# Attention of a linear-attention and feed-forward kernel rebuilt: one projection stretch a unit, four changes of array form a period

## The chip, the cores and the metric

The kernel runs on one core of one Trainium2 chip. The metric is device time in microseconds, taken as the median of three runs. The engines are TensorE (in the profile PE for matmuls and PEld for weight loads), VectorE (DVE), ScalarE (ACT), GpSimd (POOL) and SyncE (SP, which here only issues DMAs). Each engine works through its own instructions in program order and waits on semaphores for the others.

## The reference

There are 64 pairs of batch and head, with 576 positions of width 64. Keys and queries go through the same feature map, and the attention is linear: its cost grows with the sequence, not with its square. The result is rearranged to 4608 tokens of width 512 and goes through a feed-forward part whose gate is h - tanh(h).

```python
def phi(x):
    proj = np.einsum('bhsd,df->bhsf', x, w_phi)                   # d = 64, f = 128
    proj = proj - np.max(np.abs(proj), axis=-1, keepdims=True)
    return np.concatenate([np.exp(proj), np.exp(-proj)], axis=-1) # 256 features
q_p, k_p = phi(q), phi(k)
kv  = np.einsum('bhsf,bhsd->bhfd', k_p, v)
z   = np.sum(k_p, axis=2)
num = np.einsum('bhsf,bhfd->bhsd', q_p, kv)
den = np.einsum('bhsf,bhf->bhs', q_p, z)[..., None] + 1e-06
x   = (num / den), rearranged to (4608, 512)
h   = x @ w_in                                                    # (512, 2048)
out = (h - np.tanh(h)) @ w_out                                    # (2048, 512)
```

The feed-forward weights arrive as 64-bit floats and are turned to 32-bit floats on the chip ("decode").

## The kernel before, in words

**Units.** Two heads of one batch entry form a unit, so there are 32 units. For each, queries and keys stand transposed and side by side in one tile `qk` (64 rows for each head, 1152 columns: nine tiles of 128 positions). Tiles 0 to 3 and half of tile 4 are queries; the other half of tile 4 and tiles 5 to 8 are keys.

**Steps of a unit.** `project` multiplies the nine tiles by `w_phi`; the two heads sit in the upper and lower 64 rows of the array and run side by side, into the two halves (banks) of a PSUM tile. `centre` takes, on VectorE, the maximum of the absolute values over the features (`m`) and subtracts it (`t`). Keys then go through the two exponentials on ScalarE (`k_exp`, tile `kp`). Queries are first transposed on TensorE (`q_turn` and, for the half tile, `q_turn_rest`) and then go through the exponentials (`q_exp`, `q_exp_rest`, tile `qe`). `kv` multiplies keys and values (tile `pc`); its result is copied (`kv_copy`), transposed (`kv_turn`) and copied again (`kv_turn_copy`, on VectorE). `kadd` adds the key features over the five position tiles on GpSimd (tile `ss`); `ksum` adds over the 128 rows with a matmul by ones (tile `pu`), and the sum is copied, transposed and copied (`ksum_copy`, `ksum_turn`, `ksum_turn_copy`). `num` and `denom` are the products with the query features. `denom`'s result goes to memory and back in another layout (`den_recip_load`), is inverted on VectorE (`den_recip`), stored, spread over 64 rows by DMA (`den_spread`), multiplied into the numerator on GpSimd (`den_mul`) and stored (`x_store`).

**Array forms.** `project` uses the array as two tiles of 64 rows; `kv` and `num` as two of 64 columns; `denom` and `ksum` as four of 32 columns; transposes use it whole. In the profile's rows the form stands as `64*128`, `128*64`, `128*32` or `128*128`.

**Order.** `period(i)` writes the order out by hand: inside it every engine executes in the order in which the code calls. A period works on several units: unit i is projected, unit i-1 (`c`) gets its key exponentials, `kv` and query transposes, unit i-2 (`p`) its `num` and `denom`, units i-3 and i-4 the division. One weight tile is decoded in each period (`dec_0` on ScalarE, `dec_1` to `dec_3` on VectorE, in the second bank of the tile `pt`), and for 14 of them the split into a high and a low part is made too (`split_w`). The projection is in two stretches: tiles 0 to 4 at the period's start (0 to 3 into `pj`'s two banks, 4 into `pt`), tiles 5 to 8 after `kv` (into the same `pj`). The half-tile query transposes are written into `pt` as well. A first run of 16 warm-up matmuls stands ahead of unit 0's projection, a second of 16 in period 1. After 33 periods, `last` finishes the last unit, and the feed-forward part follows.

**PSUM.** Eight banks: `pj` two, `po` two single ones (used by the query transposes and by `num` in turn), `pt` two, `pc` and `pu` one each.

Of the kernel before, what the change touches and what calls it, by code (L numbers as in the profile page):

```python
# [32 lines left out]
def tile_linear_attention_moe(  # L33
# [90 lines left out]
    with ExitStack() as c1:  # L124
# [5 lines left out]
        ps_d = c1.enter_context(tc.tile_pool(name="ps_d", bufs=2, space=PSUM))  # L130
# [72 lines left out]
        def project(u, r):  # L203
            if r == 0:
                u.pt = ps_t.tile([P, 2, 512], F32, tag="pt", name=f"pt{u.i}")
                n, j0 = 5, 0
            else:
                n, j0 = 4, 5
            if (u.i, r) == (0, 1):
                pp = [ps_c.tile([P, 512], F32, tag=g, name=f"pp{u.i}_{r}_{g}") for g in ("pc", "pu")]  # L210
                u.x = [(slice(e, e + 1), slice(0, n), pp[e].rearrange("p (e a f) -> p e a f", e=1, f=F)) for e in range(2)]
            else:
                t = ps_pj.tile([P, 2, 512], F32, tag="pj", name=f"pp{u.i}_{r}")
                pp = [t[:, e, :] for e in range(2)]
                x = t.rearrange("p e (a f) -> p e a f", f=F)
                cut = (0, 4) if u.i else (0, 2, 4)
                u.x = [(slice(0, 2), slice(a0, a1), x[:, :, a0:a1]) for a0, a1 in zip(cut, cut[1:])]
                if r == 0:
                    last = (slice(0, 2), slice(4, 5), u.pt[:, :, 0:F].rearrange("p e (a f) -> p e a f", a=1))
                    u.x.insert(0 if u.i else 2, last)  # L220
            for a in range(n):
                for e in range(2):
                    hs = slice(e * D, (e + 1) * D)
                    o = u.pt[:, e, 0:F] if a == 4 else pp[e][:, a * F : (a + 1) * F]
                    nc.tensor.matmul(o, u.qk[hs, (j0 + a) * P : (j0 + a + 1) * P], wph[hs, :], start=True, stop=True)  # L225
            u.m = p2.tile([P, 2, n], F32, tag=f"m{r}", name=f"m{u.i}_{r}")
            u.t[r] = p2.tile([P, 2, n, F], F32, tag=f"t{r}", name=f"t{u.i}_{r}", bufs=1 if r else 2)

        def absmax(u, k):
            e, a, x = u.x[k]  # L230
            nc.vector.tensor_reduce(u.m[:, e, a], x, AX.X, ALU.max, apply_absolute_value=True)

        def less_max(u, r, k):
            e, a, x = u.x[k]
            m = u.m[:, e, a].unsqueeze(3).broadcast_to([P, e.stop - e.start, a.stop - a.start, F])
            nc.vector.tensor_tensor(u.t[r][:, e, a], x, m, ALU.subtract)  # L236

        def centre(u, r):
            for k in range(len(u.x)):
                absmax(u, k)  # L240
                less_max(u, r, k)

        def q_turn_rest(u, pt):
            for e in range(2):
                nc.tensor.transpose(pt[:, 0, (2 + e) * P : (3 + e) * P], u.t[0][:, e, 4, :], ident)

        def q_turn(u, e):
            pt = ps_d.tile([P, 512], F32, tag="po", name=f"ptt{u.i}_{e}")
            for j in range(4):
                nc.tensor.transpose(pt[:, j * P : (j + 1) * P], u.t[0][:, e, j, :], ident)  # L250
            return pt

        def q_exp_rest(u, pt):
            x = pt[:, 0, 2 * P : 4 * P].rearrange("p (e t) -> p e t", e=2)[:, :, 0:SR]
            for s in range(2):
                nc.scalar.activation(u.qe[:, :, s, SM:S], x, AF.Exp, scale=1.0 - 2.0 * s)

        def q_exp(u, e, pt):
            for s in range(2):
                nc.scalar.activation(u.qe[:, e, s, 0:SM], pt, AF.Exp, scale=1.0 - 2.0 * s)  # L260

        def k_exp(u, r):
            h, x, j = ((slice(SR, P), 4, 0), (slice(0, P), slice(0, 4), slice(1, 5)))[r]
            for s in range(2):
                nc.scalar.activation(u.kp[h, :, j, s, :], u.t[r][h, :, x, :], AF.Exp, scale=1.0 - 2.0 * s)  # L265
# [13 lines left out]
        def kadd(u):  # L279
            x = p1.tile([P, 2, 2, F], F32, tag="ss", name=f"ss{u.i}")  # L280
# [6 lines left out]
        def ksum(u):  # L287
            parts = [u.ss] if u.ss is not None else [u.kp[:, :, j] for j in range(5)]
            for a, x in enumerate(parts):
                for n in range(4):  # L290
                    nc.tensor.matmul(
                        u.pu[n * 32 : (n + 1) * 32, 0:F], ones, x[:, n // 2, n % 2, :], start=(a == 0), stop=(a == len(parts) - 1)
# [6 lines left out]
        def ksum_turn(u, bank, n=0):  # L299
            u.pz = bank[:, n * F : (n + 1) * F]  # L300
            nc.tensor.transpose(u.pz, u.kst, ident)

        def ksum_turn_copy(u):
            u.ks = p2.tile([P, P], F32, tag="ks", name=f"ks{u.i}")
            nc.scalar.copy(u.ks, u.pz)
# [9 lines left out]
        def num(u):  # L315
            u.po = [ps_d.tile([P, 512], F32, tag="po", name=f"po{u.i}_{c}") for c in range(2)]
            for s in range(2):
                for c in range(2):
                    for e in range(2):
                        nc.tensor.matmul(  # L320
                            u.po[c][e * D : (e + 1) * D, 0:CH],
# [20 lines left out]
        def num_copy(u):  # L342
            u.d = tail.tile([P, S], F32, tag="d", name=f"d{u.i}", bufs=2)
            for c in range(2):
                nc.scalar.copy(u.d[:, c * CH : (c + 1) * CH], u.po[c][:, 0:CH])
# [10 lines left out]
        def den_recip(u, pin=lambda ins: ins):  # L356
            w = 2 * S // P
            u.rr = dr.tile([2, S], F32, tag="rr", name=f"rr{u.i}")
            rn = tail.tile([P, w], F32, tag="rn", name=f"rn{u.i}")
            pin(nc.vector.reciprocal(rn, u.dn))  # L360
            nc.sync.dma_start(u.rr.rearrange("a s -> (a s)").rearrange("(p c) -> p c", c=w), rn)
# [14 lines left out]
        for i in range(B * NHP):  # L376
            u = Unit()
            u.i, u.b, u.hp = i, i // NHP, i % NHP
            u.t, u.ss, u.kp = {}, None, kps[i % 2]
# [6 lines left out]
        nc.scalar.dma_start(wph[D:P, :], w_phi)  # L386
        load_v(units[0])
        load(units[1])
        dec = [dec_load(0), dec_load(1)]

# [3 lines left out]
        def q_all(c, pt):  # L394
            c.qe = p2.tile([P, 2, 2, S], F32, tag="qe", name=f"qe{c.i}")
            pts = [q_turn(c, e) for e in range(2)]
            q_turn_rest(c, pt)
            if c.i:
                kv_turn(c)
            for e in range(2):  # L400
                q_exp(c, e, pts[e])
            q_exp_rest(c, pt)

        def period(i):
            a, c, p, r, q = (unit(i - n) for n in range(5))
            w = dec[i - 2] if 2 <= i < NU + 2 else None
            if q:
                den_mul(q)
                x_store(q)
            if i == NU - 2:  # L410
# [3 lines left out]
            if a:  # L414
                if i == 0:
                    warm(16, "pc")
                project(a, 0)
                pt = a.pt
                centre(a, 0)
            else:  # L420
                pt = ps_t.tile([P, 2, 512], F32, tag="pt", name=f"pt{i}")
            if i == 1:
                q_all(c, a.pt)
                warm(16, "pu")
            if p:
                num(p)
            if c:
                k_exp(c, 1)
                if i < NU:
# [267 lines left out]
```

## Time and profile before

| | us |
|---|---|
| median of three runs | 1133.14 (1131.47 to 1135.79) |
| the profiled execution | 1134.21, its span 1132.1 |
| start to the second `num` (unit 1) | 34.30 |
| from there to the `num` of unit 29, 28 periods | 277.84 |
| from there to the first feed-forward matmul | 28.49 |
| feed-forward part to the end of the span | 791.47 |

The profile is of one execution, and its times count from the start of the span. A row of the timeline is: start, length from the first to the last of a merged run, engine, line, operation, names of output and inputs, shapes, how often. A matmul of 32-bit floats leaves two records. The length of a merged run of matmuls holds the run-out of its last one, so the distance from one row's start to the next row's start says how long the array was taken. In brackets stands the idle time of the engine ahead of the run and what ended it.

### The profile page before, as it was taken

To read this page: it belongs to the slowest core of one execution; us is meant where nothing else is said; L and a number is where in the kernel's file an instruction comes from. 1 tells how busy PE (TensorE), PEld (TensorE's weight loads), DVE (VectorE), ACT (ScalarE), POOL (GpSimd) and SP (SyncE) were. 2 spreads that over 40 slices of the span, in tenths; PEclk is the share of its full clock that TensorE was granted. 3 is DMA by queue.
4 is the path that set the end of the run, shared out by engine and by line. 5 is a ranking of instruction groups with operands and counts; after the bars stand their busy time and mean duration, and the time that the engine had idled before them with its cause. 6 is when DMAs were issued, how large, how long until landed. Compare 5 with 4: busy or idle time off the path is not lost.

```text
span 1132.1 us, 18798 instructions
## 1 busy us (share of the span) xinstructions
PE 1109.2 (98%) x7008; PEld 872.2 (77%) x7008; DVE 835.6 (74%) x1170; ACT 778.9 (69%) x1488; POOL 432.3 (38%) x345
## 2 busy tenths in 40 slices
PE   7999999999979999999999999999999999999997
PEld 5666676666647888888888888888888888888885
DVE  5888888888858877767767767667676776776664
ACT  4887887777757766666666666666666666666664
POOL 4678876666634552322222222222222222222222
PEclk9999999999999999999999999999999999999999
DMA  4666767767731001101002002002002002000001
GB/s 158 179 191 212 217 207 210 208 200 216 224 103 38 1 27 48 33 21 65 1 1 75 1 1 75 1 1 75 1 1 75 1 1 75 1 1 29 10 0 38
DMA packets 51163, 85.46 MB, mean 75 GB/s; under 512 B 13312, under 2 KB 24960, under 8 KB 51072
## 3 DMA queue, kind: packets, MB, share of 16 engines
q1 hardware_dynamic: 50912, 84.20, 24.0%
q8 instruction: 55, 0.90, 0.3%
q14 instruction: 36, 0.29, 0.1%
q10 hardware_dynamic: 160, 0.07, 0.0%
HBM read 65.08 MB, written 19.02 MB: 74 GB/s over the span
## 4 chain that ended last, share of the span: by engine, by line
PE 87%; DMA 4%; POOL 3%; DVE 2%; ACT 2%; issue 1%; SPq 1%; POOLq 0%; DVEq 0%; ACTq 0%
PE ph L538 34%; PE po L581 11%; PE po L584 11%; PE po L582 11%; PE pp L225 4%; PE po L320 4%; PE pc L271 4%; PE pu L334 2%; DMA rb<-rr 2%; PE ptt L250 2%; DMA rr<-rn 2%; PE pt L225 1%; DMA dn<-dd 1%; POOL ss L282 1%; POOL ss L281 1%
## 5 line engine op out<-in xcount | busy, mean ns | idle before, releaser
L567 POOL TENSOR_TENSOR gl<-s,gh 128x512 fp32r<-128x512 f32 x144 | 186.1, 1293 | 556.2 <-ACT gh L566 547.7
L545 ACT ACTIVATE y<-ph 128x512 f32<-128x512 f32 x144 | 86.1, 598 | 254.9 <-PE ph L538 254.9
L554 DVE SCALAR_TENSOR_TENSOR s<-s,y 128x512 f32<-128x512 f32 x144 | 102.3, 711 | 187.4 <-ACT s L547 186.4
L581 PE MATMUL po<-who,gh 128*128 128x512 f32 x572 | 222.8, 389 | 1.8 <-ACT gh L566 1.8
L538 PE MATMUL ph<-xh,whi 128*128 128x512 f32 x576 | 224.3, 389 | 0.0
L538 PE MATMUL ph<-xh,wli 128*128 128x512 f32 x576 | 224.1, 389 | 0.0
L538 PE MATMUL ph<-xl,whi 128*128 128x512 f32 x576 | 224.1, 389 | 0.0
L582 PE MATMUL po<-wlo,gh 128*128 128x512 f32 x572 | 222.5, 389 | 0.0
L584 PE MATMUL po<-who,gl 128*128 128x512 f32 x572 | 152.9, 389 | 0.0
L560 DVE COPY_PREDICATED s<-mk,th 128x512 f32<-128x512 uint32 x128 | 122.9, 960 | 13.8 <-DVE th L559 0.9
L581 PEld LDWEIGHTS po<-who,gh 128*128 128x128 f32 x572 | 107.4, 188 | 24.9 <-ACT gh L566 2.6
L538 PEld LDWEIGHTS ph<-xh,whi 128*128 128x128 f32 x576 | 108.3, 188 | 23.3 <-DVE s L560 0.5
L538 PEld LDWEIGHTS ph<-xh,wli 128*128 128x128 f32 x576 | 108.1, 188 | 22.5
L538 PEld LDWEIGHTS ph<-xl,whi 128*128 128x128 f32 x576 | 108.1, 188 | 22.3
L582 PEld LDWEIGHTS po<-wlo,gh 128*128 128x128 f32 x572 | 107.4, 188 | 22.2
L584 PEld LDWEIGHTS po<-who,gl 128*128 128x128 f32 x572 | 107.3, 188 | 22.3
L547 ACT ACTIVATE s<-y,bias_t 128x512 f32<-128x512 f32 x144 | 104.4, 725 | 0.4 <-POOL gl L567 0.4
L553 ACT ACTIVATE mk<-y,bias_t 128x512 f32<-128x512 f32 x144 | 103.5, 719 | 1.4 <-DVE s L560 1.4
L557 DVE SCALAR_TENSOR_TENSOR s<-s,ph 128x512 f32<-128x512 f32 x144 | 98.9, 687 | 5.2
L556 DVE SCALAR_TENSOR_TENSOR s<-s,s 128x512 f32<-128x512 f32 x128 | 88.8, 694 | 16.2 <-ACT s L549 3.5
L265 ACT ACTIVATE kp<-t 128x1024 f32<-128x1024 f32 (+1 forms) x128 | 86.8, 727 | 14.5 <-DVE t L236 12.7
L549 ACT ACTIVATE s<-y,bias_t 128x512 f32<-128x512 f32 x128 | 92.4, 722 | 0.9 <-POOL gl L567 0.9
(101 smaller groups left out, 1708.6 us busy)
## 6 DMA issues: line engine op xcount, KB each, us to landing
qk<-in_qkT SPq DMA_DIRECT2D x31, 576.0 KB, 4.8
v<-in_v SPq DMA_DIRECT2D x32, 320.0 KB, 3.2
rb<-rr SPq DMA_DIRECT2D x64, 144.0 KB, 3.2
xs<-rb SPq DMA_DIRECT2D x32, 288.0 KB, 3.5
out<-o SPq DMA_DIRECT2D x36, 256.0 KB, 2.0
rawi<-in_moe_w_in SPq DMA_DIRECT2D x16, 512.0 KB, 3.9
rawo<-in_moe_w_out SPq DMA_DIRECT2D x16, 512.0 KB, 6.2
xl<-xs SPq DMA_DIRECT2D x24, 256.0 KB, 4.0
```

The lines of the kernel that those rows point to most:

```text
L538: nc.tensor.matmul(h, wt[:, c * P : (c + 1) * P], x[:, c, 0:N], start=(i == 0), stop=(i == 3 * NCT - 1))
L547: nc.scalar.activation(s1, y, AF.Square, bias=bias_t[:, 0:1])
L549: nc.scalar.activation(s2, y, AF.Square, bias=bias_t[:, 1:2])
L553: nc.scalar.activation(mk, y, AF.Relu, bias=bias_t[:, 2:3])
L554: nc.vector.scalar_tensor_tensor(s1, s1, PC1, y, ALU.add, ALU.mult)
L556: nc.vector.scalar_tensor_tensor(gs, s2, PC2, s1, ALU.add, ALU.mult)
L557: nc.vector.scalar_tensor_tensor(gs, gs, PA, h, ALU.mult, ALU.mult)
L560: nc.vector.copy_predicated(gs, mk.bitcast(U32), hh)
L567: pin(nc.gpsimd.tensor_tensor(gl, gs, f32(gh), ALU.subtract))
L581: nc.tensor.matmul(po[t], a, wo[f][0], start=(f == 0), stop=False)
L582: nc.tensor.matmul(po[t], a, wo[f][1], start=False, stop=False)
L584: nc.tensor.matmul(po[t], gl[:, t * P : (t + 1) * P], wo[f][0], start=False, stop=(f == NF - 1))
```

## The change

The code of the 32 units is written anew; the feed-forward part, and the order of its instructions on each engine, stay as they are.

- `project` takes a list of parts, "j" (tiles 0 to 3, into `pj`), "a" (tiles 5 to 8, into the two-bank tile `po`) and "t" (tile 4, into `pt`). A period from 4 on projects j, a and t without another step between them; period 3 in the order a, j, t.
- `num` writes one two-bank tile `po` and stands at the period's end, right behind `kv`. Its copy (`num_copy`) is one instruction. The query transposes go to `pj`, the half-tile ones to `pu`.
- `ksum_turn`, `denom`, `ksum` and the half-tile transposes of one period share a tile `pu`. `denom` is now for unit i-3 and `ksum` for unit i-2; `kadd`'s tile has two buffers.
- `q_exp` is two instructions over both heads instead of four.
- The decode's three VectorE steps stand at the period's end, behind the reciprocal; each weight tile is decoded one period later than before.
- On SP a period issues: spread of the reciprocals, v, q and k, load of the denominators, store of the reciprocals, store of x, raw weights.
- `ramp` holds the order of the first three units, `drain` that of the end. The first warm-up has 12 matmuls, the second is gone. The first unit's q and k come in two pieces instead of three. In `drain` the last unit's key sum goes through `kadd` like the others.

On TensorE, one period before (`pp` and `pt` are projection, `ptt`, `pt<-ident` and `pc<-ident` transposes, `pu<-qe` is `denom`, `pu<-ss` `ksum`):

```order
L225 MATMUL pp_0_1235<-wph,qk_1034 128x128 x8
L225 MATMUL pt_1234<-wph,qk_1034 128x128 x2
L320 MATMUL po_0_1252<-qe_1187,kv_1210 64x288 x2
...
L271 MATMUL pc_1281<-kp_113,v_1020 64x256 x10
L225 MATMUL pp_1_1308<-wph,qk_1034 128x128 x8
L301 MATMUL pu_1319<-ident,kst_1271 128x128
L250 MATMUL ptt_0_1324<-ident,t_0_1111 128x128 x4
...
L245 MATMUL pt_1234<-ident,t_0_1111 128x128 x2
L309 MATMUL pc_1281<-ident,kvt_1300 128x128 x2
L334 MATMUL pu_1319<-qe_1187,ks_1321 32x288 x8
```

and one period of the change:

```order
L219 MATMUL pj_1276<-wph,qk_1035 128x128 x8
L219 MATMUL pa_1285<-wph,qk_1035 128x128 x8
L219 MATMUL pt_1294<-wph,qk_1035 128x128 x2
L341 MATMUL pu<-qe_1084,ks_1220 32x288 x8
L299 MATMUL pu<-ss_1172,ones 32x128 x4
L316 MATMUL pc_1227<-ident,kvt_1238 128x128 x2
L247 MATMUL ptt_1334<-ident,t_0_1142 128x128 x8
L308 MATMUL pu<-ident,kst_1327 128x128
L252 MATMUL pu<-ident,t_0_1142 128x128 x2
L278 MATMUL pc_1358<-kp_114,v_1140 64x256 x10
L327 MATMUL po_1384<-qe_1215,kv_1331 64x288 x8
```

The second projection stretch has moved up to the first, `num` behind `kv`, and the transpose of `kv`'s result to the next period.

On ScalarE, in the same period of the change, from the copy of `denom` to the key exponentials that follow `num`'s copy (`kp<-t_0` and `kp<-t_1` are key exponentials, `pt<-rawi` is the decode's first step):

```order
L355 ACTIVATE dd_1192<-pu,bias_t 128x288
L305 COPY kst_1196<-pu 128x128
L171 ACTIVATE pt_1163<-rawi_989 128x512
L258 ACTIVATE qe_1215<-ptt_1203 128x2x512 x2
L267 ACTIVATE qe_1215<-pu 128x2x64 x2
L312 COPY ks_1220<-pu 128x128
L272 ACTIVATE kp_114<-t_0_1142 64x2x128 x2
L284 COPY kvt_1238<-pc_1227 128x256
L272 ACTIVATE kp_114<-t_1_1222 128x2x4x128
L351 COPY d_1262<-po_1253 128x576
L272 ACTIVATE kp_114<-t_1_1222 128x2x4x128
```

and in a period before, where the key exponentials stand ahead of the copy and in one piece:

```order
L265 ACTIVATE kp_114<-t_1_2134 128x2x4x128 x2
L265 ACTIVATE kp_113<-t_0_2199 64x2x128 x2
L297 COPY kst_2223<-pu_2135 128x128
L171 ACTIVATE pt_2186<-rawi_2046 128x512
L345 COPY d_2226<-po_0_2204 128x288
L345 COPY d_2226<-po_1_2205 128x288
L277 COPY kvt_2252<-pc_2233 128x256
```

The copy of `num` has moved between the two long key exponentials of the unit that was just projected.

The diff, without the new `ramp` and `drain` past their heads:

```diff
-        ps_d = c1.enter_context(tc.tile_pool(name="ps_d", bufs=2, space=PSUM))
+        ps_d = c1.enter_context(tc.tile_pool(name="ps_d", bufs=1, space=PSUM))
...
-            cut = (0, PC) if u.i else (0, 2 * P, 5 * P, PC)
+            cut = (0, PC) if u.i else (0, 4 * P, PC)
...
+        def project(u, parts):
+            for part in parts:
+                if part == "j":
...
+                    u.pj = ps_pj.tile([P, 2, 512], F32, tag="pj", name=f"pj{u.i}")
+                    bank, tiles = u.pj, range(4)
+                elif part == "t":
+                    u.pt = ps_t.tile([P, 2, 512], F32, tag="pt", name=f"pt{u.i}")
+                    bank, tiles = u.pt, range(4, 5)
+                else:
+                    u.pa = ps_d.tile([P, 2, 512], F32, tag="po", name=f"pa{u.i}")
+                    bank, tiles = u.pa, range(5, 9)
+                for k, a in enumerate(tiles):
+                    for e in range(2):
+                        hs = slice(e * D, (e + 1) * D)
+                        nc.tensor.matmul(
+                            bank[:, e, k * F : (k + 1) * F], u.qk[hs, a * P : (a + 1) * P], wph[hs, :], start=True, stop=True
+                        )
...
+        def centre(u, parts):
+            for part in parts:
+                x, m, t = part_of(u, part)
+                nc.vector.tensor_reduce(m, x, AX.X, ALU.max, apply_absolute_value=True)
+                nc.vector.tensor_tensor(t, x, m.unsqueeze(3).broadcast_to(list(t.shape)), ALU.subtract)
...
+        def num(u, pool=ps_d, tag="po"):
+            u.po = pool.tile([P, 2, 512], F32, tag=tag, name=f"po{u.i}")
...
         def num_copy(u):
             u.d = tail.tile([P, S], F32, tag="d", name=f"d{u.i}", bufs=2)
-            for c in range(2):
-                nc.scalar.copy(u.d[:, c * CH : (c + 1) * CH], u.po[c][:, 0:CH])
+            nc.scalar.copy(u.d.rearrange("p (c n) -> p c n", c=2), u.po[:, :, 0:CH])
...
+        def ramp():
+            a, b, c = units[0:3]
+            warm(12, "pc")
+            project(a, "jat")
...
         def period(i):
             a, c, p, r, q = (unit(i - n) for n in range(5))
-            w = dec[i - 2] if 2 <= i < NU + 2 else None
+            w = dec[i - 3]
+            low = split_w(i - 4) if 4 <= i < 2 * AHEAD + 4 else None
+            if q:
+                den_spread(q)
+            if i > 3:
+                load_v(a)
+            project(a, "jat" if i > 3 else "ajt")
+            if i + 2 < NU:
+                load(units[i + 2])
+            centre(a, "jt")
+            kadd(c)
             if q:
                 den_mul(q)
+            if low:
+                low()
+            pu = bank()
+            if r:
+                denom(r, pu)
+            ksum(p, pu)
+            if r:
+                denom_copy(r)
+                den_recip_load(r)
+            ksum_copy(p)
+            kv_turn(p)
+            kv_turn_copy(p)
+            dec_0(w, a.pt)
+            q_turn(c)
+            ksum_turn(p)
+            q_turn_rest(c, pu)
+            q_exp(c)
+            q_exp_rest(c)
+            ksum_turn_copy(p)
+            centre(a, "a")
+            k_exp(a, 0)
+            kv(c)
+            kv_copy(c)
+            k_exp(a, 1, (0,))
+            if r:
+                den_recip(r)
+                den_store(r)
+            if q:
                 x_store(q)
+            dec_1(w)
+            dec_2(w)
+            dec_3(w)
+            dec.append(dec_load(i - 1))
...
+            num(p)
+            num_copy(p)
+            k_exp(a, 1, (1,))
...
+        def drain():
+            q, r, p, c = units[-4:]
+            kadd(c)
...
+            kv(c)
+            num(p)
...
+            kv_turn(c)
...
+            ksum(c, pu)
+            denom(p, pu)
...
+            ksum_turn(c)
...
+            num(c)
...
+            denom(c, bank())
+            denom_copy(c)
```

More of the change, by code (lines that the diff above doesn't have):

```diff
@@ L243, in q_turn_rest @@
[L243 to L254, printed above, removed]
+        def project(u, parts):
+            for part in parts:
+                if part == "j":
+                    u.t = [p2.tile([P, 2, 5, F], F32, tag="t0", name=f"t{u.i}_0"), None]
+                    u.m = [p2.tile([P, 2, 5], F32, tag="m0", name=f"m{u.i}_0"), p2.tile([P, 2, 4], F32, tag="m1", name=f"m{u.i}_1")]
+                    u.pj = ps_pj.tile([P, 2, 512], F32, tag="pj", name=f"pj{u.i}")
[12 more added lines that the diff above has]
+                        )
@@ L386, in tile_linear_attention_moe, with bank @@
         nc.scalar.dma_start(wph[D:P, :], w_phi)
+        load(units[1])
         load_v(units[0])
-        load(units[1])
-        dec = [dec_load(0), dec_load(1)]
+        load_v(units[1])
+        dec = []
         def unit(i):
             return units[i] if 0 <= i < NU else None
[L394 to L402, printed above, removed]
+        def bank():
+            return ps_c.tile([P, 512], F32, tag="pu", name="pu")
@@ new lines, in ramp @@
+        def ramp():
+            a, b, c = units[0:3]
+            warm(12, "pc")
+            project(a, "jat")
+            load(c)
+            dec.extend(dec_load(n) for n in range(2))
+            centre(a, "jta")
+            k_exp(a, 0)
+            q_turn(a, ("pc", "pu"))
+            q_turn_rest(a, a.pt[:, 0])
+            project(b, "j")
+            q_exp(a)
+            q_exp_rest(a)
+            k_exp(a, 1)
+            project(b, "at")
+            load(units[3])
+            centre(b, "jta")
+            kadd(a)
+            q_turn(b)
+            k_exp(b, 0)
+            kv(a)
+            load_v(c)
+            q_turn_rest(b, b.pt[:, 0])
+            q_exp(b)
+            kv_copy(a)
+            q_exp_rest(b)
+            kv_turn(a)
+            kv_turn_copy(a)
+            project(c, "jat")
+            load(units[4])
+            k_exp(b, 1)
+            centre(c, "jta")
+            kadd(b)
+            pu = bank()
+            ksum(a, pu)
+            ksum_copy(a)
+            kv(b)
+            load_v(units[3])
+            kv_copy(b)
+            ksum_turn(a)
+            ksum_turn_copy(a)
+            k_exp(c, 0)
+            k_exp(c, 1, (0,))
+            num(a, ps_pj, "pj")
+            num_copy(a)
+            k_exp(c, 1, (1,))
@@ L413, in period @@
                     x_load(0, xt[0], j)
[L414 to L429, printed above, removed]
-                    kadd(c)
@@ L500, in last, with decode @@
+        def decode(w):
+            pt = ps_t.tile([P, 2, 512], F32, tag="pt", name="pt")
+            dec_0(w, pt)
             dec_1(w)
@@ L507, in tile_linear_attention_moe @@
         with tc.manual_schedule():
-            for i in range(NU + 1):
+            ramp()
+            for i in range(3, NU):
                 period(i)
-            last()
-        den_recip_load(units[-2])
-        den_mul(units[-3])
-        x_store(units[-3])
+            drain()
         den_recip_load(units[-1])
```

209 lines of the change are left out of this document (88 added, 121 removed).

## The prediction

> **What bounds the kernel now.** I read the page first, then the windows by stage, then one period of the attention engine by engine. On the page, the busy times and the chain that ended last:
>
> ```profile
> PE 1109.2 (98%) x7008; PEld 872.2 (77%) x7008; DVE 835.6 (74%) x1170; ACT 778.9 (69%) x1488; POOL 432.3 (38%) x345
> ...
> PE 87%; DMA 4%; POOL 3%; DVE 2%; ACT 2%; issue 1%; SPq 1%; POOLq 0%; DVEq 0%; ACTq 0%
> ```
>
> TensorE is the bound nearly everywhere. By stages (length, then busy time of PE, PEld, DVE, ACT, POOL, then granted clock), cut at the second `num`, at that of unit 29 and at the first matmul of the feed-forward part:
>
> ```profile
> 34.30:312.14 277.84, 274.84 (x3055) 190.41 (x3053) 243.21 (x336) 220.44 (x492) 197.25 (x153) 1.00 0.69 207
> 312.14:340.63 28.49, 22.03 (x229) 13.58 (x228) 14.50 (x22) 17.11 (x40) 9.27 (x7) 0.94 0.35 102
> 340.63:1132.10 791.47, 785.15 (x3460) 648.39 (x3456) 557.20 (x783) 525.19 (x926) 213.61 (x164) 1.00 0.07 25
> ```
>
> The last row is 70% of the span; its instructions and their order stay, so I leave it at 791.5. The first row is 28 periods of 277.84/28 = 9.92 us each. The second is the drain, with 6.5 us of idle TensorE. Now one period on TensorE (start, length, work):
>
> ```profile
> 200.35 1.18 PE L334 MATMUL pu<-qe,ks 128*32 128x288 f32 x16
> 201.34 0.40 PE L291 MATMUL pu<-ss,ones 128*32 128x128 f32 x8
> 201.67 1.16 PE L225 MATMUL pp<-wph,qk 64*128 64x128 f32 x16
> 202.85 0.49 PE L225 MATMUL pt<-wph,qk 64*128 64x128 f32 x4
> 203.27 2.16 PE L320 MATMUL po<-qe,kv 128*64 128x288 f32 x16
> 205.26 2.33 PE L271 MATMUL pc<-kp,v 128*64 128x256 f32 x20
> 207.52 1.16 PE L225 MATMUL pp<-wph,qk 64*128 64x128 f32 x16
> 208.62 0.33 PE L301 MATMUL pu<-ident,kst 128*128 128x128 f32 x1
> 208.78 1.04 PE L250 MATMUL ptt<-ident,t 128*128 128x128 f32 x8
> ...
> 209.88 0.38 PE L309 MATMUL pc<-ident,kvt 128*128 128x128 f32 x2
> 210.19 1.18 PE L334 MATMUL pu<-qe,ks 128*32 128x288 f32 x16
> ```
>
> The array forms are in the column with the star: 32-column, 64-row, 64-column, 64-row, full, 32-column: five changes in 9.84 us.
>
> **Price of a change of form.** The pace inside one form shows in unit 0's second projection, first and last of eight pairs, and above them the first projection of all:
>
> ```profile
> 4.62 1.16 PE L225 MATMUL pp<-wph,qk 64*128 64x128 f32 x16
> ...
> 5.83 0.27 PE L225 MATMUL pp_pc<-wph,qk 64*128 64x128 f32 x1
> ...
> 6.62 0.27 PE L225 MATMUL pp_pc<-wph,qk 64*128 64x128 f32 x1
> ```
>
> Seven steps in 0.79 us are 0.112 a pair, so eight pairs need 0.89; the stretch at 207.52 takes 1.10 to the next start. Entering and leaving the form cost 0.21. Likewise two transposes at 209.88 take 0.31 to the next start where the ten before them run at 0.11 each: 0.09 for that change.
>
> **The period after.** Projection is one stretch (18 pairs, 2.02), then `denom` and `ksum`, 13 transposes, `kv` and `num`; four changes. Against 9.84: the second stretch's 0.21 goes. In the first stretch ten pairs, 1.12, should with entry and exit take 1.31; they take 1.60 (201.67 to 203.27). The 0.29 between is a wait, and DVE shows for what:
>
> ```profile
> 201.31 0.41 DVE L313 COPY kv<-pc 128x256 f32<-128x256 f32 x1
> 202.02 0.69 DVE L183 SCALAR_TENSOR_TENSOR wo<-rawo,pt 128x512 uint32<-128x512 uint32 x1 [0.29 <-ACT qe L256]
> 203.38 0.42 DVE L231 TENSOR_REDUCE m<-pt 128x2 f32<-128x256 f32 x1 [0.68 <-PE pt L225]
> ...
> 204.18 1.22 DVE L231 TENSOR_REDUCE m<-pp 128x8 f32<-128x1024 f32 x1
> 205.43 1.23 DVE L236 TENSOR_TENSOR t<-pp,m 128x1024 f32<-128x1024 f32 x1
> 206.57 0.20 DVE L360 RECIPROCAL rn<-dn 128x9 f32<-128x9 f32 x1
> ```
>
> The decode's last step (L183) ends at 202.71, held by the exponentials that read the same tile; the projection into `pt` starts at 202.85. In the change those exponentials read `pu`, and tile t comes last in the stretch, so this wait should go. TensorE's own work is then 9.84 - 0.21 - 0.29 = 9.34.
>
> But three hand-overs now lie inside the round. I count from T, the first projection matmul. TensorE: part a at T+1.0, t at 1.9, `denom` 2.2, `kv_turn` 3.6, `q_turn` 3.8, `kv` 5.1, `num` 7.3, next T at 9.3. DVE starts when part j is complete, T+1.2, and steps as above: maximum 1.25, subtraction 1.14, the pair for t 0.80, `kv` copy 0.33 and again 1.25 + 1.2. Part j's bank is empty at T+3.7, with 0.1 to TensorE at 3.8, exactly when `q_turn` wants it; part a's at T+7.2, when `num` wants it. Reciprocal and decode end at T+10.0, 1.2 ahead of the next t. ScalarE:
>
> ```profile
> 202.26 2.82 ACT L265 ACTIVATE kp<-t 128x1024 f32<-128x1024 f32 x4
> ...
> 205.39 0.67 ACT L171 ACTIVATE pt<-rawi 128x512 f32<-128x512 f32 x1
> 205.98 0.70 ACT L345 COPY d<-po 128x288 f32<-128x288 f32 x2
> 207.64 0.37 ACT L277 COPY kvt<-pc 128x256 f32<-128x256 f32 x1 [0.96 <-PE pc L271]
> 208.98 0.27 ACT L305 COPY ks<-pu 128x128 f32<-128x128 f32 x1 [0.97 <-PE pu L301]
> 209.42 2.06 ACT L260 ACTIVATE qe<-ptt 128x512 f32<-128x512 f32 x4 [0.17 <-PE ptt L250]
> 211.34 0.48 ACT L256 ACTIVATE qe<-pt 128x128 f32<-128x128 f32 x2
> ```
>
> From t's subtraction (done T+4.5) it runs decode 0.67, `q_exp` 2.06, the rest 0.48, 0.27, the first three key exponentials (some 1.8 of the 2.82), 0.37, less about 0.6 of overlap (2.06 from 209.42 ends 0.14 past 211.34): T+9.5. `num` is done at 9.4. The copy out of `po`, about 0.65 as one instruction, ends at T+10.15, 0.85 into the next round, where part a wants that bank at 1.0. So all three meet within 0.1. A bank's hand-over costs 0.14 (202.71 to 202.85). None missed: 9.34; each missed by 0.14: 9.76. I take 9.45, a third of the way, because the rows I count with already hold their latencies. 28 x (9.92 - 9.45) = **13.2 us**, bounds 4.5 and 16.2. Every 0.1 us in this figure is 2.8 us in the end. POOL carries what it carries now, 197.25/28 = 7.0 us a period, and its key sum has until the next period's `ksum` instead of the same one's. Of the moved transfers, the spread of the reciprocals is issued on SP behind the raw weights, whose load waits for the decode's end at T+10.0, so at T+1.3 of the next round; POOL wants it after its sums, at about T+6.8, and ScalarE the buffer that POOL then frees at T+9.4. The loads of q, k and v behind it are for units one and two rounds away. I cost these at nothing, since 5 us of POOL's sums cover the spread; without that cover POOL's product, then the copy out of `po`, would come late.
>
> **The ramp.** It is a chain through DVE. Unit 0's part j is complete at 4.62 + 1.16 = 5.8, as now; its centring takes 2.39 + 0.80 + 2.39, to 11.4; unit 1's j to 13.8; `q_turn` 1.0, ScalarE's 2.0 beside `kv` 2.3, copy and turn 0.8, so unit 2 is projected from 17.9 and complete at 19.0, centred at 24.6. Key exponential 1.0 and copy 0.7: 26.4, where unit 3's j finds its bank free. It is complete at 27.6 and centred at 33.5, where the second `num` starts; it is 34.30 now. With hand-overs I call it equal: **0**, bounds 2 gained and 3 lost.
>
> **The drain.** From unit 29's `num`: its 2.0, `denom` and `ksum` 1.3, transposes 1.6, `kv` 2.2, `num` 2.0, `kv_turn` 0.35, `ksum` and `denom` 1.3, turning the last sum 0.9, `num` 2.0, `denom` 1.1: 14.75, with 1 us for waits 15.7 against 28.49. What goes is in these rows:
>
> ```profile
> 322.70 0.42 PE L291 MATMUL pu<-ss,ones 128*32 128x128 f32 x8 [2.20 <-POOL ss L284]
> ...
> 332.24 0.47 PE L301 MATMUL pt<-ident,kst 128*128 128x128 f32 x1 [3.38 <-DVE pt L179]
> 332.51 1.91 PE L250 MATMUL ptt<-ident,t 128*128 128x128 f32 x8
> ```
>
> These three rows hold 5.6 us of waiting, and the last one a halved clock (1.91 for what took 1.04), good for 1.7. Of the busy time, unit 30's `kv` 2.26, its transposes 1.57 and one projection stretch 1.10 now stand ahead of the cut, and the last unit's key sum is made by POOL, which leaves 4 matmuls instead of 20 (some 1.0 at 0.05 each). Together 13.2, near the 12.8 of the two sums. Gain **12.8**, bounds 13.7 (no waits at all) and 8 (the old waits of 5.6 stay, less what is covered). POOL's last sum can start when ScalarE has unit 31's keys, 3.7 after the cut, takes 5.1 and is wanted at 9.4; without these 0.6 us of cover TensorE waits.
>
> **Sum.** -13.2 + 0 - 12.8 = -26.0. The profiled execution took 1134.21 us (span 1132.1), the median run 1133.14, 1.1 less: 1107 to 1108.
>
> **Rivals.**
>
> 1. The hand-overs bind: DVE's ring and TensorE wait for each other and the period is 9.75. For it: no slack in three places; against it: the sums are worked from rows with latency. 28 x 0.17 = 4.8, drain 10: about 1118.
>
> 2. The ramp runs at half clock. It drops the second warm-up and 4 of the first 16.
>
> ```profile
> 21.24 0.63 PE L291 MATMUL pu<-ss,ones 128*32 128x128 f32 x8 [1.98 <-POOL ss L284]
> 21.80 2.08 PE L225 MATMUL pp<-wph,qk 64*128 64x128 f32 x16
> ...
> 21.80:24.23 2.43, 2.43 (x24) 2.21 (x20) 0.03 (x1) 1.74 (x2) 0.56 (x1) 0.50 0.18 72
> ```
>
> After 1.98 us of idleness the clock is 0.50 and sixteen projections take 2.08 instead of 1.16. By the chain above TensorE waits in the new ramp from 6.8 to 8.3, from 10.5 to 11.5 and from 12.6 to 13.9, each shorter than this one. If two of them bring a halved stretch as long as here, about 3 us, some 1.5 is lost in each: 1111. The Trainium skill, "TensorE: Matmul & The Clock Gate", section "Why this matters for your kernels", asks for no idle gap over about 3 us; by that rule no wait of this ramp would slow the clock and the ramp stays at my number, but the row at 21.24 speaks against it.
>
> 3. Slower: the reciprocal waits for its DMA. It stands ahead of the decode on DVE, and now its load is issued behind the spread, v and the next q and k:
>
> ```profile
> 202.40 0.59 SPq L354 DMA_DIRECT2D dn<-dd  x1
> ...
> DVE rn L360 <- DMA dn<-dd: 1.2, 2, 0.8
> ```
>
> Now 4.2 us from issue to use (202.40 to 206.57) cover it, with two waits in 28 periods. Then it is issued at T+4.1 and wanted at T+7.1: 3.0, plus DVE's 0.5 of idle time. Landing after 5 us would stretch every period by 1.5, to 10.95: 28 x 1.03 = 29 lost, 13 gained in the drain: 1150. It turns the whole slower from about 4.4 us on. Against it: q and k's load was in flight in these rows too.
>
> **Chances.** Forecast 0.58 (own range 1101 to 1114), hand-overs 0.23, clock 0.10, reciprocal 0.06, others 0.03. Range 1099 (period 9.34, ramp 2 better, drain at its bound) to 1122 (period 9.76, drain 8). A measurement here tells 0.5% from no change; faster by more 0.91, within 0.03, slower 0.06.
>
> **What would show it.** Projection rows of 16, 16 and 4 back to back, without a gap ahead of `pt`; four forms a period; starts of `num` 9.4 to 9.5 us apart. Waits of TensorE on DVE ahead of `q_turn` or `num` mean rival 1; a clock of 0.50 between 8 and 26 us rival 2; DVE idle ahead of the reciprocal rival 3. First `num` of unit 1 near 34, first feed-forward matmul near 315. It is wrong if the period stays above 9.7 or the drain above 20.

## Result: slower by 2.7%, where 2.2% faster was forecast

The changed kernel takes 1164.65 us (median of four runs, 1163.37 to 1165.66), the kernel before 1133.28 beside it: a ratio of 1.0275, interval 1.0252 to 1.0297. The prediction was 1108, range 1099 to 1122. Of its three rivals the third, to which it gave 0.06, is what happened.

Windows of the changed kernel, cut at the same places as before (length, then busy time of PE, PEld, DVE, ACT, POOL with instruction counts, granted clock, DMA share, GB/s):

```profile
37.80:351.58 313.78, 277.77 (x3055) 187.51 (x3054) 243.59 (x336) 213.19 (x407) 199.04 (x153) 0.99 0.60 181
351.58:370.31 18.73, 16.32 (x150) 8.81 (x149) 11.60 (x19) 11.88 (x25) 8.74 (x7) 0.91 0.54 149
370.31:1162.30 791.99, 785.22 (x3460) 648.18 (x3456) 558.80 (x786) 526.59 (x928) 214.04 (x165) 1.00 0.07 25
```

| us | before | predicted | changed | best repair (below) |
|---|---|---|---|---|
| start to the second `num` | 34.30 | 34.3 | 37.80 | 34.81 |
| 28 periods | 277.84 | 264.6 | 313.78 | 264.21 |
| one period | 9.92 | 9.45 | 11.21 | 9.44 |
| drain | 28.49 | 15.7 | 18.73 | 17.90 |
| feed-forward | 791.47 | 791.5 | 791.99 | 791.88 |
| span | 1132.1 | 1106 | 1162.3 | 1108.8 |

Most of the loss is in the second row: 35.9 us more in 28 periods; 3.5 more go in the ramp, and 9.8 are gained in the drain. In the 28 periods TensorE was busy for 274.84 of 277.84 us before; now it idles for 36. The chain that ended last, on the page of the changed kernel:

```profile
PE 72%; DMA 14%; DVE 10%; ACT 2%; issue 1%; SPq 1%; POOL 0%; POOLq 0%; ACTq 0%; DVEq 0%
```

DMA went from 4% to 14% of it, and 12% is `dn`, the load of the denominators, 4.5 KB a period. The waits in the 28 periods (total, how often, longest):

```profile
DVE rn L365 <- DMA dn<-dd: 59.4, 27, 3.3
...
PE pt L219 <- DVE wi L183: 20.7, 13, 2.2
```

Before there were two such waits of the reciprocal, of 1.2 us together; now it waits in 27 of 28 periods, 2.2 us each. One turn, on VectorE, then SP, then TensorE:

```profile
218.11 0.21 DVE L365 RECIPROCAL rn<-dn 128x9 f32<-128x9 f32 x1 [2.68 <-DMA dn<-dd]
...
220.42 0.69 DVE L183 SCALAR_TENSOR_TENSOR wi<-rawi,pt 128x512 uint32<-128x512 uint32 x1
...
225.86 1.23 DVE L236 TENSOR_TENSOR t<-pa,m 128x1024 f32<-128x1024 f32 x1
229.18 0.21 DVE L365 RECIPROCAL rn<-dn 128x9 f32<-128x9 f32 x1 [2.10 <-DMA dn<-dd]
```

```profile
221.17 0.38 SPq L159 DMA_DIRECT2D rawi<-in_moe_w_in  x1
221.60 2.12 SPq L375 DMA_DIRECT2D rb<-rr  x2
223.82 0.53 SPq L200 DMA_DIRECT2D v<-in_v  x1
224.45 0.38 SPq L196 DMA_DIRECT2D qk<-in_qkT  x1
224.92 0.59 SPq L360 DMA_DIRECT2D dn<-dd  x1
```

```profile
230.22 1.06 PE L219 MATMUL pa<-wph,qk 64*128 64x128 f32 x16
232.23 0.49 PE L219 MATMUL pt<-wph,qk 64*128 64x128 f32 x4 [0.94 <-DVE wo L183]
```

The turn closes on itself. The reciprocal at 218.11 lets the decode run to its end at 221.1. That frees the raw weights' buffer, so SP issues their load at 221.17 (3.06 later), then spread, v, q and k without a pause, and `dn` at 224.92 (3.75 later). The next reciprocal starts at 229.18 (4.26 later). 3.06 + 3.75 + 4.26 = 11.07, where TensorE needs 9.4. TensorE pays at the projection into `pt`: it shares the tile with the decode, and the decode stands behind the late reciprocal.

### The profile page after: what moved, and what is told of

The parts are those of the page before. It is cut to its first block, busy times and chain, and to the rows that moved or that the text cites. A ratio compares the mean times of both kernels' runs of the same rounds, so it can differ in the third digit from the quotient of the medians.

```text
span 1162.3 us, 18558 instructions
## 1 busy us (share of the span) xinstructions
PE 1109.3 (95%) x6956; PEld 866.5 (75%) x6956; DVE 837.1 (72%) x1166; ACT 771.1 (66%) x1394; POOL 439.2 (38%) x349
## 4 chain that ended last, share of the span: by engine, by line
PE 72%; DMA 14%; DVE 10%; ACT 2%; issue 1%; SPq 1%; POOL 0%; POOLq 0%; ACTq 0%; DVEq 0%
PE ph L599 33%; DMA dn<-dd 12%; PE po L642 11%; PE po L645 11%; PE po L643 11%; PE pu L341 2%; DVE pt L179 2%; DVE pt L176 2%; DVE t L236 1%; DVE m L235 1%; DVE pt L175 1%; PE pt L219 1%; DVE wi L183 1%; DVE wo L183 1%; PE pc L316 1%
## 5 line engine op out<-in xcount | busy, mean ns | idle before, releaser
L272 ACT ACTIVATE kp<-t 128x1024 f32<-128x1024 f32 (+1 forms) x128 | 90.5, 731 | 11.7 <-DVE t L236 10.5
```

## The experiments

Two theories. A: the period is long because the reciprocal, ahead of the decode on VectorE, waits for `dn`. B: the hand-overs of banks between TensorE, VectorE and ScalarE bind (the prediction's first rival), and the wait for `dn` only fills slack. Ratios are to the kernel before on the same chip; a period is the time from unit 1's `num` to unit 29's, divided by 28.

### The wait taken away

```diff
-            pin(nc.vector.reciprocal(u.rn, u.dn))
+            pin(nc.vector.reciprocal(u.rn, cd if u.i < NU - 4 else u.dn))
```

`cd` is a tile that is filled once with a constant, so this kernel leaves out the division by the true denominators.

> The reciprocal of all but the last four units reads a tile filled once with a constant instead of the loaded denominators; the load is still issued, and everything else stands as in the change. It leaves out the division by the true denominators, so that only VectorE's wait for that load is gone. Theory A (the changed kernel is slow because the reciprocal, which stands ahead of the decode on VectorE, waits for its load): the period falls from 11.21 to 9.4-9.6 us, the time from 1164.6 to 1114-1121. Theory B (the hand-overs of banks between TensorE, VectorE and ScalarE bind, and the wait for the load is only where the slack is spent): the period stays above 10.5 and the time above 1143.

Measured: 1114.41 us, ratio 0.9812 (0.9783 to 0.9840). The 28 periods, and one of them on TensorE:

```profile
38.36:302.69 264.33, 264.19 (x3055) 183.55 (x3054) 243.32 (x336) 211.40 (x407) 198.80 (x153) 1.00 0.72 215
```

```profile
200.73 1.16 PE L221 MATMUL pj<-wph,qk 64*128 64x128 f32 x16
201.73 1.06 PE L221 MATMUL pa<-wph,qk 64*128 64x128 f32 x16
202.62 0.39 PE L221 MATMUL pt<-wph,qk 64*128 64x128 f32 x4
202.94 1.18 PE L343 MATMUL pu<-qe,ks 128*32 128x288 f32 x16
```

264.33/28 = 9.44 us with TensorE busy for 264.19 of it. Theory A holds and B falls: 49.5 us of the 313.78 hang on this one wait, and without it no hand-over holds the array up. The gain is more than the 36 us in which TensorE idled: its busy time falls by 13.6 us too (277.77 to 264.19). Part of these are two stretches at half clock in the changed kernel's periods (last section); the rest was not traced.

### Three ways to have the wait met

The reciprocal behind the decode:

```diff
             k_exp(a, 1, (0,))
+            dec_1(w)
+            dec_2(w)
+            dec_3(w)
             if r:
                 den_recip(r)
...
             if q:
                 x_store(q)
-            dec_1(w)
-            dec_2(w)
-            dec_3(w)
```

> The reciprocal, its store and the store of x stand behind the decode's three steps instead of ahead of them; nothing else changes, the output is the same. Theory A: the load gets 2.9 us more, VectorE's wait goes, period 9.4-9.6, time 1114-1121, as long as the later spread of the reciprocals still comes before GpSimd wants it (about 6.8 us into the next period; I reckon it at 5.5). Theory B: above 1143. If the spread comes late instead, GpSimd waits for rb and the time is 1125-1143.

The raw weights behind `dn`:

```diff
                 den_recip_load(r)
+            if i > 3:
+                dec.append(dec_load(i - 2))
...
             dec_3(w)
-            dec.append(dec_load(i - 1))
```

> The load of the raw weights is issued on SP right behind the load of the denominators of the next period instead of ahead of it; it keeps its buffer and still has nearly a period until it is used. Theory A with the lateness coming from the transfers issued ahead: one of them, 512 KB, is gone, the load lands some 2.5 us earlier than now, VectorE's wait falls from 2.2 us a period to 0-0.5: period 9.4-9.8, time 1114-1126. If it is not the order of issue but the load on the DMA engines as such, the wait stays near 2 and the time above 1155. Theory B: above 1143.

`dn` from another queue:

```diff
-                den_recip_load(r)
+                den_recip_load(r, nc.scalar)
...
```

> The load of the denominators is issued from ScalarE's queue, right behind the copy that it reads, instead of from SP's; order and bytes of all other transfers stay. If its lateness is the queue (its packets stand behind the bulk transfers issued on SP before it), it lands within about 2 us, VectorE's wait goes, period 9.4-9.7, time 1114-1124. If the DMA engines themselves hold it up whatever the queue, it lands as late as now (about 4 us) and the time stays within 1150-1168.

Measured: 1127.58 (ratio 0.9934, 0.9910 to 0.9958), 1116.23 (0.9838, 0.9812 to 0.9864) and 1158.97 (1.021, 1.018 to 1.024); periods 278.09/28 = 9.93, 266.86/28 = 9.53 and 307.81/28 = 10.99.

Behind the decode, the waits between 40 and 300 us show the third outcome of its expectation:

```profile
POOL rb L379 <- DMA rb<-rr: 27.1, 18, 3.1
...
ACT d L351 <- POOL rb L379: 12.0, 11, 2.2
```

GpSimd waited for the spread in the change too (45.2 us between 40 and 300 us), but ScalarE's copy out of `po` then waited for GpSimd only once, for 0.6 us. Now that copy waits for the buffer that GpSimd frees 11 times, and VectorE still waits for `dn` for 10.7 us. So the reciprocal's place is not the cure: behind the decode it is late for its next user.

Moving one 512 KB transfer behind the small one is nearly the whole cure: it gives back 47 of the 49.5 us. A queue of its own is none:

```profile
211.02 0.55 ACTq L360 DMA_DIRECT2D dn<-dd  x1
```

```profile
217.13 0.21 DVE L365 RECIPROCAL rn<-dn 128x9 f32<-128x9 f32 x1 [2.61 <-DMA dn<-dd]
```

Here `dn` is issued right behind the copy it reads and still reaches the reciprocal 6.1 us later, with 2.6 us of waiting. Over the 28 periods VectorE waits for it 25 times, 53.3 us in all. A place of its own in another queue does not help while SP's bulk loads are in flight. The Trainium skill, "DMA: Bandwidth & Descriptors", section "Issuing engines are not separate DMA queues", says that transfers of all issuers run on the same 16 DMA engines and interleave; this run fits the first half of that. Its section "Queues, rings and completion order" has each engine take turns between its queues at packet granularity; by that a 4.5 KB load alone in its queue would land early, and here it did not.

### Which bytes, and who else is small

Only q and k behind `dn` (raw weights where the change has them):

```diff
-            if i + 2 < NU:
-                load(units[i + 2])
...
                 den_recip_load(r)
+            if i + 2 < NU:
+                load(units[i + 2])
```

> Only the load of the next q and k (576 KB) is moved on SP behind the load of the denominators; the raw weights stay ahead of it as in the change. Theory A1 (the small load comes after the bytes that were issued before it, whichever they are): it should land 2.5-3 us earlier, VectorE's wait mostly goes, period 9.4-9.8, time 1114-1126. Theory A2 (what matters is the place of the raw weights, whose load SP holds until the decode is done, so that everything behind it is issued late): the period stays above 10.5, the time above 1143.

Both behind `dn`, with the head of the ramp put back (its diff is further down):

> All three repairs together: raw weights and next q and k both issued behind the load of the denominators, and the head of the ramp as before. Nothing bulky but v and the spread is then ahead of the small load. Period 9.42 (what TensorE alone needs), second num near 34.5, drain 16: time 1110, against 1133 before and 1164.6 for the change. If the bytes now queued behind it make v, the spread or the raw weights late instead, GpSimd or the decode waits and the time is above 1116.

Measured: 1124.50 (ratio 0.9903, 0.9881 to 0.9926; period 271.30/28 = 9.69) and 1125.22 (0.9912, 0.9892 to 0.9933; period 280.59/28 = 10.02). The first says that 576 KB less ahead of `dn` helps too, whichever bytes they are: A1, not A2. The second was meant to be the best, and its period is longer than with either move alone (9.53 and 9.69). Its waits on SP, and on VectorE:

```profile
SPq L375 <- DMA rr<-rn: 98.1, 25, 6.2
```

```profile
DVE rn L365 <- DMA dn<-dd: 25.7, 21, 3.0
```

There is a second small transfer in the ring: `rr`, the store of the reciprocals, 4.5 KB, 3 us behind `dn`. Now 1088 KB (512 and 576) go out just ahead of it; SP waits 3.9 us a period for it to land, and issues the spread, v and everything behind them late. Theory C: both small transfers must find the DMA engines idle. The raw weights behind `rr`, q and k behind `dn`:

```diff
                 den_recip_load(r)
+            if i + 2 < NU:
+                load(units[i + 2])
...
                 den_store(r)
+            if i > 3:
+                dec.append(dec_load(i - 2))
```

> As the kernel with all three repairs, but the raw weights are issued right behind the store of the reciprocals, and the next q and k stay behind the load of the denominators. Theory C (every small transfer comes after the bytes issued before it, so each of the two small ones, dn and rr, must find the engines idle): dn, issued 4.1 us into a period, has only v and the spread of 4 us earlier ahead of it; rr, issued at 7.4, only q and k of 3 us earlier; SP no longer waits long for rr. Period 9.42-9.48, second num near 34.6, drain 16, time 1109-1112, under every kernel so far. If the small transfers are late for another reason (the wait of SP for rr as such, or the total load of 2.0 MB a period), the period stays at 9.5 or above and the time above 1112.

And both behind `rr`:

> As the one before, but q and k too are issued behind the store of the reciprocals (raw weights, then q and k: 1.06 MB at 7.4 us into the period). rr finds the engines idle; the spread, v and then dn come behind the 1.06 MB. At the 0.2-0.25 MB per us that the profiles show these take 4-5 us, to about 2.5 us into the next period, v and the spread (0.6 MB) 2.5 more, to 5.0, so dn, issued at 4.1, lands some 1 us late: VectorE waits 0-0.5 us, period 9.45-9.8, time 1111-1120. If only the order on SP mattered and not the bytes, period 9.42 and 1110.

Measured: 1111.01 (1110.62 to 1111.21), ratio 0.9787 (0.9763 to 0.9811), the best of all; and 1134.38 for the second, ratio 0.9998 (0.9983 to 1.0013). Windows and SP's wait of the first:

```profile
34.81:299.02 264.21, 264.05 (x3054) 183.69 (x3054) 243.42 (x336) 211.04 (x408) 198.57 (x153) 1.00 0.73 214
299.02:316.92 17.90, 14.71 (x151) 8.02 (x149) 10.66 (x19) 11.69 (x25) 8.79 (x7) 1.00 0.61 173
```

```profile
SPq L375 <- DMA rr<-rn: 18.6, 22, 1.8
```

Same bytes, same instructions: one split of the two bulk loads gives 9.44 us a period, another 10.22 (286.07/28). In the second, both ends of the ring are late:

```profile
POOL rb L379 <- DMA rb<-rr: 35.9, 24, 2.6
...
DVE rn L365 <- DMA dn<-dd: 30.7, 24, 2.7
```

My number for it missed: I divided the bytes ahead by the mean rate and got up to 0.5 us of waiting; it was 1.3 each time, and I had not followed the spread, which lands 6.8 us after its issue there (median) and 4.6 in the best order. The direction and the place of the waits came as said; the price by the mean rate was too low here.

### The price of a change of form

```diff
-            project(a, "jat" if i > 3 else "ajt")
+            pu = bank()
+            if i > 4:
+                project(a, "j")
+                denom(r, pu)
+                project(a, "at")
+            else:
+                project(a, "jat" if i > 3 else "ajt")
...
-            pu = bank()
-            if r:
+            if r and i <= 4:
                 denom(r, pu)
             ksum(p, pu)
```

> On the kernel with the constant in place of the denominators (1114.4 us, period 9.44, TensorE without a gap), denom is put between the first eight and the last ten pairs of the projection, so a period has two projection stretches and six changes of form instead of four; the number of matmuls is the same. By the price in the prediction (0.21 us for entering and leaving the 64-row form once more) the period becomes 9.65 and the time 1114.4 + 27 x 0.21 = 1120. If a change of form costs nothing, or lies in slack, the period stays at 9.44 and the time at 1113-1116.

Measured: 1122.31 (1120.15 to 1123.02) against 1114.41 without it, ratio to before 0.9885 (0.9864 to 0.9906, the other's was 0.9783 to 0.9840). The windows of the 28 periods and the rows of one:

```profile
38.85:310.03 271.18, 271.18 (x3054) 185.68 (x3054) 244.29 (x336) 212.28 (x407) 198.90 (x153) 1.00 0.70 210
```

```profile
205.37 1.16 PE L221 MATMUL pj<-wph,qk 64*128 64x128 f32 x16
206.46 1.18 PE L343 MATMUL pu<-qe,ks 128*32 128x288 f32 x16
207.56 1.16 PE L221 MATMUL pa<-wph,qk 64*128 64x128 f32 x16
208.56 0.39 PE L221 MATMUL pt<-wph,qk 64*128 64x128 f32 x4
208.88 0.42 PE L301 MATMUL pu<-ss,ones 128*32 128x128 f32 x8
```

271.18/28 = 9.685 against 9.44: 0.245 us for two more changes (0.25 in the 27 periods that have them), where I had 0.21. Part j is taken for 1.09 instead of 1.00, `denom` for 1.10 instead of 0.99: about a tenth at each end of a form.

### The head of the ramp

```diff
-            cut = (0, PC) if u.i else (0, 4 * P, PC)
+            cut = (0, PC) if u.i else (0, 2 * P, 5 * P, PC)
...
-        load(units[1])
         load_v(units[0])
-        load_v(units[1])
+        load(units[1])
...
-            warm(12, "pc")
+            warm(16, "pc")
...
-            load(c)
             dec.extend(dec_load(n) for n in range(2))
+            load_v(b)
+            load(c)
```

> On the kernel with the raw weights loaded later (1116.2 us), the head of the ramp is put back: 16 warm-up matmuls, three pieces of the first q and k, v of unit 0 ahead of q and k of unit 1, v of unit 1 behind the first raw weights. Theory A for the ramp (the first projection waits for the second half of wph, which comes behind larger pieces, and then runs at half clock): the first projection starts near 4.6 instead of 6.7, the second num near 34.5 instead of 37.2, time about 1113.5. Theory B (the ramp's chain is bound elsewhere, or the clock halves in its later gaps all the same): second num stays at 36.5-37.5 and the time at 1115-1117.

The best order with 12 warm-up matmuls again:

> As the first of these three, with 12 warm-up matmuls instead of 16, which is what the change has; the first loads stay in the repaired order. If the half clock in the changed kernel's ramp came from the wait for wph, nothing changes: second num near 34.6 and the time within 1 us of the first one. If it is the number of warm-up matmuls, a half-clock stretch shows before 20 us and the second num comes 1-2 us later.

Measured: 1112.68 (ratio 0.9802, 0.9779 to 0.9826) and 1111.56 (0.9794, 0.9765 to 0.9823; the same as with 16). The second `num` starts at 34.81 and 34.97. What the head cost, in rows of the changed kernel and its clock from 7.75 to 11.16, and then the same two steps with the head put back:

```profile
4.06 0.60 PE L219 MATMUL pj<-wph,qk 64*128 64x128 f32 x2
7.49 1.66 PE L219 MATMUL pj<-wph,qk 64*128 64x128 f32 x13 [2.83 <-DMA wph<-in_w_phi]
9.39 1.23 DVE L235 TENSOR_REDUCE m<-pj 128x8 f32<-128x1024 f32 x1 [8.49 <-PE pj L219]
```

```profile
7.75:11.16 3.41, 3.41 (x34) 3.41 (x32) 1.73 (x2) 0.00 (x0) 0.00 (x0) 0.50 0.16 65
```

```profile
4.91 1.45 PE L219 MATMUL pj<-wph,qk 64*128 64x128 f32 x16
6.40 1.23 DVE L235 TENSOR_REDUCE m<-pj 128x8 f32<-128x1024 f32 x1 [5.50 <-PE pj L219]
```

The first projection stops after its first pair: the second half of `w_phi`, issued from ScalarE's queue, is not there. That looks like the same fault a third time, a small load beside larger pieces of q and k; which of the changed loads it was is not separated. 2.83 us of idleness and one stretch at clock 0.50 follow, and with the loads in the old order both are gone. VectorE's first maximum starts 3.0 us later (9.39 against 6.40), and so does the second `num` (37.80 against 34.81): the ramp is the chain through VectorE, and it is 28.4 us from the one to the other in both.

The same head stands in six of the experiments above (the constant, the four orders without a new head, the two stretches). There the wait for `w_phi` is 0.8 to 2.8 us and the second `num` starts between 36.3 and 39.4. In three of them (the constant, the reciprocal behind the decode, the other queue) the next unit's projection is slow as well, and VectorE waits for it another 1.0 to 1.4 us; in the one with the constant:

```profile
13.39 2.08 PE L221 MATMUL pj<-wph,qk 64*128 64x128 f32 x16
```

That is the pace of half clock (16 in 2.08 instead of 1.16, as in the prediction's row at 21.80), although the column of the granted clock reads 1.00 from 6.35 to 15.40 there. At the start of the span, go by the pace of the rows. With the loads in the old order 12 warm-up matmuls do as well as 16; 16 with the change's order were not tried.

### The last raw weights

```diff
                 den_recip_load(r)
+            if i == NU - 1:
+                dec.append(dec_load(i - 2))
...
-            if i > 3:
+            if 3 < i < NU - 1:
                 dec.append(dec_load(i - 2))
```

> As the 1111.0 us kernel, but the raw weights that the last period loads are issued behind the load of the denominators instead of behind the store of the reciprocals, 3 us earlier (no q and k are left to load there). In that kernel the drain took 17.9 us against 15.9 where this load was issued at the earlier place, with 2.2 us of waiting of ScalarE for these weights. If that wait is the cause, the drain falls to 16.0 and the time to 1109. If the drain's length is set by the other waits that the profile shows there (GpSimd for the spread, VectorE for dn), it stays at 17-18 and the time at 1111.

Measured: 1111.82 (1110.55 to 1113.64), ratio 0.9802 (0.9776 to 0.9827): not to be told from the 1111.01. The drain did fall, to 16.24; the second `num` came 0.6 later in this execution.

## Why the prediction was wrong

- **The step that failed** is the sentence on the moved transfers, "I cost these at nothing". It followed the spread to its user and stopped; what the moved raw weights do to the load of the denominators was left to the third rival, and dismissed there with "q and k's load was in flight in these rows too". The term put at nothing measured 49.5 us: VectorE waits 2.2 us for `dn` in 27 of 28 periods, and without that wait the periods are at the forecast. Those rows had v, the spread, q and k ahead of `dn`; the raw weights stood behind it. The 4.2 us that I read there were the time the load had, not the time it took, and a change that cuts the one needs the other.
- **What could have been worked out.** The issues with their sizes (KB each, median us to landing) stood on the page of the kernel before:

```profile
qk<-in_qkT SPq DMA_DIRECT2D x31, 576.0 KB, 4.8
v<-in_v SPq DMA_DIRECT2D x32, 320.0 KB, 3.2
rb<-rr SPq DMA_DIRECT2D x64, 144.0 KB, 3.2
...
rawi<-in_moe_w_in SPq DMA_DIRECT2D x16, 512.0 KB, 3.9
```

  In the change's order 512 + 2 x 144 + 320 + 576 = 1696 KB, 1.74 million bytes, go out ahead of `dn`, from about T+0.7 on. At the 207 GB/s of the prediction's first windows row that is an estimated 8.4 us, to T+9.1, where the reciprocal wanted `dn` at T+7.1 and had 0.5 to spare: 1.5 late, the rival's own figure. In the turn shown above it took 8.0 us from the issue of the raw weights to the reciprocal (221.17 to 229.18). The rival was the sum by bytes; it should have been the forecast.
- **The rival's price** was 10.95 a period and 1150. The period measured 11.21: the ring also holds SP's issue of five transfers, 3.75 us in the turn shown, which the rival left out. The time measured 1164.65: against that rival's sum the periods lost 7 us more, the ramp 3.5, and the drain gained 9.8 instead of 13.
- **The miss, added up** from the table: 49.2 in the 28 periods, 3.5 in the ramp, 3.0 in the drain, 0.5 in the feed-forward part, 56.2 together. From 1108 that gives the 1164.2 of the profiled execution.
- **The period without the wait**: forecast 9.45, measured 9.44, and that is in part luck. The forecast was 9.34 of TensorE's own work and 0.11 for hand-overs. Measured, TensorE is busy for 264.19 of 264.33 us, so the hand-overs cost nothing (rival 1 falls), and its own work is 9.42 in most periods. The 9.34 was worked out from one period of 9.84, where the mean of the 28 is 9.92; the two errors cancel. The price of a form was 0.245 for 0.21.
- **The ramp**: called equal, bound 3 lost; it lost 3.5, of which 3.0 come back with the head put back, where the second `num` starts at 34.6 to 35.4, against 34.30 before. I had not followed the second half of `w_phi` either. Rival 2's sign, half clock in the ramp, did show, behind the wait for `w_phi`; the fewer warm-up matmuls that it also blamed cost nothing once the loads were in the old order.
- **The drain**: forecast 15.7; 15.9 in the three kernels with the raw weights right behind `dn`, 18.73 in the change. Row by row there (ScalarE, GpSimd, TensorE):

```profile
356.04 0.64 ACT L351 COPY d<-po 128x576 f32<-128x576 f32 x1 [2.10 <-POOL rb L379]
```

```profile
354.59 1.41 POOL L379 TENSOR_TENSOR rb<-d,rb 128x576 f32<-128x576 f32 x1 [3.16 <-DMA rb<-rr]
```

```profile
358.24 0.33 PE L308 MATMUL pu<-ident,kst 128*128 128x128 f32 x1 [1.98 <-ACT kst L305]
...
358.71 3.98 PE L278 MATMUL pc<-kp,v 128*64 128x256 f32 x20
```

  The late spread holds GpSimd, that ScalarE's copy, that TensorE for 1.98 us, and behind the gap 20 matmuls take 3.98 instead of 2.38. This is the chain that the prediction named as the price "without that cover".
- **Feed-forward**: 791.99 for 791.5, as said.

With its transfers put in another order and the old head of the ramp, the change comes to 1111.01 for a predicted 1108, 2.1% under the kernel before.

## What to carry to other kernels

Before moving a bulk transfer, list the small ones that somebody waits for, and for each add up the bytes issued ahead of it; divided by the rate in the profile this gives a first estimate of the time until it lands (8.4 us for a measured 8.0 in the change; about 1 us too little in the order with both loads behind `rr`), and it belongs beside the time until it is wanted. In this kernel it paid to place bulk loads right behind a small transfer, split so that the next small one finds them gone; another queue did not replace that. And a wait that is absent from a profile has a margin that the profile does not show: the time to the use is not the time to the landing.

## What the runs showed of the chip

A 4.5 KB load alone in its queue took 6.1 us from issue to use (211.02 to 217.13, above) while bulk loads were in flight from another queue. In the best order, with the bulk out of the way, it was there within 2.94 us, without a wait:

```profile
201.67 0.59 SPq L360 DMA_DIRECT2D dn<-dd  x1
```

```profile
204.61 0.21 DVE L365 RECIPROCAL rn<-dn 128x9 f32<-128x9 f32 x1
```

Why the turns that the queues take did not help it was not tried and stays open.

The clock halved behind some idle gaps of TensorE and not behind others of the same length. Two of the changed kernel's periods:

```profile
86.12 0.70 PE L219 MATMUL pt<-wph,qk 64*128 64x128 f32 x4 [1.95 <-DVE wi L183]
86.75 2.15 PE L341 MATMUL pu<-qe,ks 128*32 128x288 f32 x16
...
336.13 0.49 PE L219 MATMUL pt<-wph,qk 64*128 64x128 f32 x4 [2.19 <-DVE wi L183]
336.56 1.18 PE L341 MATMUL pu<-qe,ks 128*32 128x288 f32 x16
```

Behind 1.95 us the clock was 0.50 for 3.41 us, and the 16 matmuls took 2.15; behind 2.19 us it stayed at 1.00, and they took 1.18. In the other runs half clock followed gaps as short as 1.00 us (ramp of the kernel with two stretches, at 17.02, with another gap of 0.81 us ahead of it at 14.62) and 1.75 us (drain with `dn` from the other queue), and it did not follow one of 2.57 us (drain with the reciprocal behind the decode). So the length of one gap does not decide it in that range; what does was not found.

The Trainium skill, "TensorE: Matmul & The Clock Gate", section "Why this matters for your kernels", asks for no idle gap over about 3 us. Keeping to that was not enough here: gaps of 1.75, 1.95, 1.98 and 2.83 us, each under that bound, were followed by half clock.
